# Attention and two feed-forward layers on one core: the second chunk's keys through GpSimd, keys ahead of queries, the second weight by halves

## The chip, the cores and the metric

The kernel runs on one core of a Trainium2 chip. The metric is device time in microseconds (us), median of several executions; lower is better. The core has five engines that each carry out their own list of instructions in order: TensorE (PE, matrix products), VectorE (DVE), ScalarE (ACT), GpSimd (POOL) and SyncE (SP, which here only issues DMAs). An engine waits at an instruction until the semaphores that it names are there, and everything behind it in that engine's list waits too.

## What is computed

```python
def _attn_ref(q, k, v):                       # (8, 8, 576, 64) each
    q_s = np.exp(q - np.max(q, axis=-1, keepdims=True))
    q_s = q_s / (np.sum(q_s, axis=-1, keepdims=True) + 1e-09)
    k_s = np.exp(k - np.max(k, axis=2, keepdims=True))
    k_s = k_s / (np.sum(k_s, axis=2, keepdims=True) + 1e-09)
    kv = np.einsum('bhsd,bhse->bhde', k_s, v)
    return np.einsum('bhsd,bhde->bhse', q_s, kv).astype(np.float32)

def _moe_ref(x, w_in, w_out):                 # x (4608, 512), d_ff 2048
    h = x @ w_in
    return (np.maximum(0.01 * h, h) @ w_out).astype(np.float32)

def _moe2_ref(x, w1, w2, w3, w_out):          # d_ff 768
    h = np.maximum(np.maximum(x @ w1, x @ w2), x @ w3)
    return (h @ w_out).astype(np.float32)
```

The weights come as float64, so a kernel reads them as pairs of 32-bit words. Queries are normalised along the 64 numbers of a head, keys along the 576 rows of the sequence.

## The kernel before

The 4608 rows are cut into nine chunks of 512. Attention makes the rows of a chunk (`x`), the first layer (A) takes them through 16 slices of its weights (`m` = 0 to 15), the second layer (B) follows at the end. Products are made from a high and a low half of each operand, three products for one (`mm3`, L639).

**Units.** A batch `b` has four key units (`kv_unit`), one for each pair of heads `hp`, and a chunk `c` has four query units (`q_unit`). A key unit loads keys `ke` and values `vt` (L400, L404 or L451), finds the maximum of each column of the keys over all rows, takes the exponential, multiplies keys by values (L461) and puts the result, divided by the sums, into `plain` (L471). A query unit loads `qt` (L513), finds maxima and sums along each head (L534 to L557), transposes `qt` on PE (L563), copies the transposed tile to `qf` (L565) and multiplies it by `plain` (L571). `split_x` then makes the halves of `x`: the high one on ACT (L613), the low one partly through a product of PE with minus the high half (L619) and a copy by ACT (L620), partly by DVE (L623). A unit is a generator: each `yield` ends a stage, and `advance` or `background` takes every unit one stage further.

**The maxima of keys.** In the first two batches PE transposes the keys (L415, five products a unit), and DVE finds the maxima along the free axis (L420, L421). In batch 0 the exponential is taken on the transposed tile; in batch 1 (`b == 1`) the maxima are put on a diagonal (L426) and spread over partitions by a product with the all-ones tile `ones` (L429), before DVE adds them to the keys (L431). From batch 2 on DVE takes maxima of the five key blocks (L444, L446), GpSimd's `partition_all_reduce` (L447) does it over partitions, and DVE subtracts (L452).

**Order at the start.** Units of batch 0 and chunk 0 run first, then weight 0 is converted, then the units of chunk 1 take two stages, and their others stand around step 0 of the loop over `turns`. A step is one slice `m` for one chunk: project (L639, 12 products into one PSUM tile), `g` (L917, ACT), `split_g` (L659 ACT, L660 DVE), `background(step)`, then `a_out` of the step before (12 products). The first steps are chunk 0 with m=0, then chunk 1 with m=0 and 1, then chunk 0 with m=1, 2, 3.

**Weights.** Each slice is converted by `split_words`: ACT takes the absolute value into the one scratch tile `ca` (L172, `Abs`), DVE works on it (L173 to L175), ACT writes the high half (L177), DVE goes on (L178, L179, L184) and writes the low half (L185), ACT copies a part back (L188) and issues its store (L189). `ca` has one buffer, so the conversions follow one another. `conv_a(m, after)` of slices 3 to 15 is called at steps `BEGUN` = (0, 0, 0, 2, 3, 5, 7, ... 25), and L171 has it wait for that step's `g`.

**Values.** From chunk 3 on (`CONV` = 3) the units take the number n = 4(b − 3) + hp. Their values go to a tile `vt` of a pool with one buffer, or to the tile `plain`, which is free by then: `plain` for odd n above 2.

**What sets the order.** The tile scheduler orders the instructions of each engine when the program is built; `pin` holds some in the order of the code. So an edit in one place can move instructions elsewhere.

Of the kernel before, what the change touches and what calls it, by code (L numbers as in the profile page):

```python
# [71 lines left out]
def tile_kernel(ctx: ExitStack, tc: tile.TileContext, q, k, v, wa, wb, out):  # L72
# [34 lines left out]
    def psum():  # L107
        return ps.tile([P, N], F32, tag="ps", name="ps")
# [13 lines left out]
    ones = const.tile([P, P], F32, name="ones")  # L122
# [32 lines left out]
    def split_words(raw, hi, lo, n, after=None, whole=None, keep=None):  # L155
# [30 lines left out]
        if keep is not None:  # L186
            copy = raw.bitcast(F32)[:, :N]
            nc.scalar.activation(copy, af[:, :N], AF.Copy)  # L188
            pin(nc.scalar.dma_start(keep, copy))  # L189

# [165 lines left out]
    nc.gpsimd.memset(plain, 0.0)  # L356
    spares = {}
# [26 lines left out]
    def kv_unit(b, hp, early):  # L384
# [22 lines left out]
        if b < FIRST:  # L407

            t4, t1 = (ps_acc.tile([P, N], F32, tag="acc", name="t") if i == b == 0 else psum() for i in range(2))
# [13 lines left out]
            if b == 1:  # L423

                diag = ap.tile([P, P], F32, tag="mx", name="diag", bufs=2)
                nc.scalar.activation(diag, ident, AF.Copy, scale=mx[:, 0:1])  # L426
                yield
                spread = psum()
                nc.tensor.matmul(spread[:, :P], lhsT=ones, rhs=diag, start=True, stop=True)  # L429
                yield  # L430
                nc.vector.tensor_tensor(ke, ke, spread[:, None, :P].to_broadcast([P, RK, P]), op=ALU.add)  # L431
                nc.scalar.activation(ke, ke, AF.Exp)
            else:
                nc.scalar.activation(back[:, :N], t4, AF.Exp, bias=mx[:, 0:1])
                nc.scalar.activation(back[:, N:], t1[:, :P], AF.Exp, bias=mx[:, 0:1])
                yield
                transposes()
                yield
                nc.scalar.activation(back[:, :N], t4, AF.Copy)
                nc.scalar.activation(back[:, N:], t1[:, :P], AF.Copy)  # L440
        else:
            mx = ap.tile([P, P], F32, tag="mx", name="mx", bufs=2)
            behind_step(mx[:, 0:1])
            nc.vector.tensor_tensor(mx, ke[:, 0], ke[:, 1], op=ALU.max)  # L444
            for r in range(2, RK):
                nc.vector.tensor_tensor(mx, mx, ke[:, r], op=ALU.max)  # L446
# [4 lines left out]
            fetch.dma_start(vt, v[b, hp])  # L451
# [54 lines left out]
    def q_unit(c, hp, early):  # L506
# [52 lines left out]
        qf = ap.tile([P, N], F32, tag=("qf", "qhi", "qlo")[hp % 3] if early else "qf", name="qf", bufs=1)  # L559
# [171 lines left out]

    def plan_units(c):
# [643 lines left out]
```

## Time and profile before

| | |
|---|---|
| median of three runs | 1404.0 us (1402.93, 1404.0, 1405.25) |
| profiled execution | 1404.38 us, of which the span from the first to the last instruction is 1402.6 us |
| busy over the span | PE 1380.4 us (98%), DVE 866.1 (62%), ACT 673.7 (48%), POOL 156.1 (11%) |
| chain that ended last | PE 91%, DVE 5%, ACT 2%, issue 1%, DMA 1% |
| granted TensorE clock | 0.997 of full speed as a mean |

How to read it: a share of the span says how much work an engine has, not what the time hangs on. PE is busy almost throughout, so time is lost or won where PE is not busy, or where its clock is granted at a lower level. The start (to 53.4 us) and the stretch of the weights' conversion (to some 200 us) are read by stretches and timelines below.

### The profile page before, as it was taken

The page shows a single profiled execution, that of the slowest core. Times are in us where ns is not written, and L with a number is a line of the kernel's source. Part 1 is how long each engine was busy: PE and PEld are TensorE (multiplying, and loading weights), DVE is VectorE, ACT ScalarE, POOL GpSimd, SP SyncE. Part 2 cuts the span into 40 slices and gives each one's busy share as a digit, 9 for nine tenths or more (in the row PEclk, how much of TensorE's full clock was granted, in tenths as well). Part 3 has the DMA queues.
Part 4 walks back from the last instruction along what each step waited for, and adds up shares of the span by engine and source line. Part 5 has one row for each costly group of instructions (what it writes and reads, how often), then busy time and mean ns, then how long its engine had stood idle before and what let it go on. Part 6 is the DMA issues. An engine that isn't in the chain of part 4 may idle for free.

```text
span 1402.6 us, 18333 instructions
## 1 busy us (share of the span) xinstructions
PE 1380.4 (98%) x6624; PEld 1129.5 (81%) x6624; DVE 866.1 (62%) x1500; ACT 673.7 (48%) x1387; POOL 156.1 (11%) x261
## 2 busy tenths in 40 slices
PE   7999999999999999999999999999999999999998
PEld 5788877888888788888888888888888888888887
DVE  9888977864786884656647455666457255434311
ACT  7766867753776755655445344334224223322211
POOL 0000202200112130210223200110010000000000
PEclk9999999999999999999999999999999999999999
DMA  9388864635977966768788797664674573454601
GB/s 368 129 282 302 302 225 131 199 101 213 381 291 272 374 207 230 284 219 348 243 336 335 275 372 259 243 226 172 219 268 136 210 293 120 169 221 157 235 29 38
DMA packets 90826, 330.10 MB, mean 235 GB/s; under 512 B 10672, under 2 KB 27056, under 8 KB 67568
## 3 DMA queue, kind: packets, MB, share of 16 engines
q1 hardware_dynamic: 68512, 251.46, 48.7%
q0 software_dynamic: 19056, 66.98, 14.2%
q10 hardware_dynamic: 3168, 10.49, 1.9%
q8 instruction: 52, 0.85, 0.2%
q14 instruction: 38, 0.31, 0.1%
HBM read 253.66 MB, written 75.24 MB: 234 GB/s over the span
## 4 chain that ended last, share of the span: by engine, by line
PE 91%; DVE 5%; ACT 2%; issue 1%; DMA 1%; SPq 0%; DVEq 0%; POOL 0%; ACTq 0%
PE ps L867 40%; PE acc L639 35%; PE ps L639 13%; PE ps L591 1%; PE ps L461 1%; DVE glo L660 0%; DVE qmx L534 0%; DVE side L832 0%; DVE qsm L549 0%; DMA spare<-in_q_dram 0%; DMA vt<-in_v_dram 0%; DVE nmx L420 0%; DVE spare L557 0%; PE ps L571 0%; ACT qo L527 0%
## 5 line engine op out<-in xcount | busy, mean ns | idle before, releaser
L867 PE MATMUL ps<-op,group 128*128 128x512 f32 x1512 | 352.2, 389 | 0.0
L867 PEld LDWEIGHTS ps<-op,group 128*128 128x128 f32 x1512 | 283.8, 188 | 59.0 <-ACT snap L1099 0.2
L639 PE MATMUL acc<-ghi,outw 128*128 128x512 f32 x768 | 248.2, 391 | 0.9 <-ACT ghi L659 0.5
L867 PE MATMUL ps<-opA,group 128*128 128x512 f32 x1008 | 247.4, 391 | 0.6 <-ACT opA L827 0.6
L867 PEld LDWEIGHTS ps<-opA,group 128*128 128x128 f32 x1008 | 188.0, 188 | 41.1 <-ACT opA L827 1.0
L639 PEld LDWEIGHTS acc<-ghi,outw 128*128 128x128 f32 x768 | 143.8, 188 | 32.1 <-ACT ghi L659 1.6
L639 PE MATMUL acc<-glo,outw 128*128 128x512 f32 x384 | 150.6, 392 | 0.6 <-DVE glo L660 0.2
L639 PE MATMUL acc<-wo,h 128*128 128x512 f32 x558 | 135.6, 389 | 0.0
L639 PE MATMUL ps<-xhi,w 128*128 128x512 f32 x384 | 127.1, 398 | 1.3 <-ACT g L917 0.7
L639 PE MATMUL acc<-ghi,w 128*128 128x512 f32 x384 | 127.2, 394 | 0.0
L1099 ACT ACTIVATE snap<-ps 128x512 f32<-128x512 f32 x108 | 61.8, 596 | 134.6 <-PE ps L867 134.3
L639 PEld LDWEIGHTS acc<-wo,h 128*128 128x128 f32 x558 | 104.8, 188 | 21.7
L660 DVE TENSOR_TENSOR glo<-g,ghi 128x512 fp32r<-128x512 f32 x102 | 69.5, 686 | 74.4 <-ACT ghi L659 74.1
L1114 DVE TENSOR_TENSOR snap<-snap,ps 128x512 f32<-128x512 f32 x72 | 49.1, 684 | 92.8 <-ACT snap L1099 69.4
L639 PEld LDWEIGHTS ps<-xhi,w 128*128 128x128 f32 x384 | 72.8, 190 | 17.8 <-ACT g L917 1.1
L639 PEld LDWEIGHTS acc<-glo,outw 128*128 128x128 f32 x384 | 72.1, 188 | 17.2 <-DVE glo L660 2.5
L659 ACT ACTIVATE ghi<-g 128x512 fp32r<-128x512 f32 x102 | 63.4, 630 | 46.0 <-DVE g L1299 27.3
L639 PEld LDWEIGHTS acc<-ghi,w 128*128 128x128 f32 x384 | 71.9, 188 | 15.4
L1110 DVE TENSOR_TENSOR best<-snap,ps 128x512 f32<-128x512 f32 x36 | 24.7, 686 | 87.7 <-PE ps L867 38.8
L639 PE MATMUL ps<-xlo,w 128*128 128x512 f32 x192 | 75.5, 394 | 0.0
L639 PE MATMUL acc<-glo,w 128*128 128x512 f32 x192 | 75.3, 392 | 0.0
L1123 ACT ACTIVATE h<-best 128x512 fp32r<-128x512 f32 x48 | 30.3, 630 | 87.5 <-DVE best L1116 87.1
(188 smaller groups left out, 1916.0 us busy)
## 6 DMA issues: line engine op xcount, KB each, us to landing
group<-stream SPq DMA_DIRECT2D x62, 1024.0 KB, 6.6
outw<-stream_out SPq DMA_DIRECT2D x48, 1024.0 KB, 8.4
group<-stream_in SPq DMA_DIRECT2D x42, 1024.0 KB, 7.8
stream<-room POOLq DMA_DIRECT2D x66, 256.0 KB, 5.5
raw<-in_wa_dram SPq DMA_DIRECT2D x16, 1024.0 KB, 7.7
x<-st SPq DMA_DIRECT2D x40, 256.0 KB, 3.3
room<-in_wb_dram POOLq DMA_DIRECT2D x18, 512.0 KB, 8.0
stream_out<-w SPq DMA_DIRECT2D x16, 512.0 KB, 3.5
```

The lines of the kernel that those rows point to most:

```text
L461: nc.tensor.matmul(acc[z, : D + 1], lhsT=ke[:, r, z], rhs=vt[:, r, h], start=r == 0, stop=r == RK - 1)
L591: nc.tensor.matmul(both(xps, c0, c1), lhsT=a, rhs=halves(y, c0, c1), start=i == 0, stop=i == 2)
L639: nc.tensor.matmul(acc, lhsT=l, rhs=r, start=first and i == 0, stop=last and i == 2)
L659: nc.scalar.activation(hi[:, z], g[:, z], AF.Copy)
L660: nc.vector.tensor_tensor(lo[:, z], g[:, z], hi[:, z].bitcast(F32), op=ALU.subtract)
L867: nc.tensor.matmul(bank, lhsT=l, rhs=r, start=fresh and first, stop=last, skip_group_check=not fresh)
L1099: nc.scalar.activation(t, bank, AF.Copy)
L1110: nc.vector.tensor_tensor(g, snap, bank, op=ALU.add)
L1114: nc.vector.tensor_tensor(snap, snap, bank, op=ALU.add)
L1123: nc.scalar.activation(h[:, m, 0], g, AF.Copy)
```

## The change

It has five parts, all in the code for the first 230 us.

1. Keys of batch 1 no longer pass through PE. DVE takes the maximum over the five key blocks in one reduction over a strided view (L457 of the new file, `ke.rearrange("p r d -> p d r")`), GpSimd reduces over partitions (L463), DVE subtracts (L469). The 20 transposes, the diagonals and the four products with `ones` go. `ones` shrinks to one column, and a first `partition_all_reduce` on it is issued at the start (L380).
2. For chunk 1 all four key units stand ahead of the four query units in the list of units, and after step 0 the query units are taken on pair by pair.
3. The second weight (m=1) is converted by `split_by_halves`: ACT's `Abs` (L195) around step 0, then DVE does two halves of eight operations (L201 to L208; the high half too, L204), between the query units' stages. The third weight follows with the old function.
4. `qf` of chunks 0 and 1 goes back into `qt`'s place instead of three tiles of the pool.
5. Values of units n = 2, 4, 6, ... go to `plain`, where before n = 3, 5, 7, ... did.

```diff
+    def split_by_halves(raw, hi, lo, keep):
+        words = raw.bitcast(U32).rearrange("p (n t) -> p n t", t=2)
+        a = cp.tile([P, 2 * N], U32, tag="ca", name="ca")
+        pin(nc.scalar.activation(a.bitcast(F32), words[:, :, 1].bitcast(F32), AF.Abs))
+        yield
+        for i in range(2):
+            z = slice(i * N, i * N + N)
...
+            pin(nc.vector.tensor_scalar(af, af, MOST_HIGH, LEAST_HIGH, op0=ALU.min, op1=ALU.max))
...
+            nc.vector.tensor_copy(hi[:, z], af)
...
+            nc.vector.tensor_tensor(lo[:, z], af, hi[:, z].bitcast(F32), op=ALU.subtract)
+        yield
+        copy = raw.bitcast(F32)[:, :N]
+        pin(nc.scalar.activation(copy, a.bitcast(F32)[:, :N], AF.Copy))
+        pin(nc.scalar.dma_start(keep, copy))
...
+    pin(nc.gpsimd.partition_all_reduce(ones, ones, P, bass_isa.ReduceOp.max))
...
-            if n % 2 and n > 2:
+            if n > 1 and n % 2 == 0:
                 vt = plain.rearrange("p a n -> p (a n)")[:, : RK * 2 * (D + 1)]
...
-        if b < FIRST:
+        if b == 0:
...
-            if b == 1:
-
-                diag = ap.tile([P, P], F32, tag="mx", name="diag", bufs=2)
-                nc.scalar.activation(diag, ident, AF.Copy, scale=mx[:, 0:1])
-                yield
-                spread = psum()
-                nc.tensor.matmul(spread[:, :P], lhsT=ones, rhs=diag, start=True, stop=True)
-                yield
-                nc.vector.tensor_tensor(ke, ke, spread[:, None, :P].to_broadcast([P, RK, P]), op=ALU.add)
-                nc.scalar.activation(ke, ke, AF.Exp)
...
             mx = ap.tile([P, P], F32, tag="mx", name="mx", bufs=2)
...
+            if b < FIRST:
+                nc.vector.tensor_reduce(mx, ke.rearrange("p r d -> p d r"), axis=AX.X, op=ALU.max)
+            else:
+                behind_step(mx[:, 0:1])
...
-        qf = ap.tile([P, N], F32, tag=("qf", "qhi", "qlo")[hp % 3] if early else "qf", name="qf", bufs=1)
+        if c < FIRST:
+            qf = qt
+        else:
+            qf = ap.tile([P, N], F32, tag=("qf", "qhi", "qlo")[hp % 3] if early else "qf", name="qf", bufs=1)
...
-    second = advance(first_units(1), 2)
+    second = [unit(1, hp, True) for unit in (kv_unit, q_unit) for hp in range(NP)]
+    advance(second[:NP], 2)
+    advance(second[NP:], 2)
...
+            if step == 0:
+                convert = conv_by_halves(1)
+                next(convert)
             background(step)
...
             if step == 0:
-                second = advance(second, 2)
+                advance(second[:NP])
+                for hp in range(NP):
+                    advance(second[NP : NP + hp + 1], 2)
                 a_out(*prev, hold=True)
                 prev = None
-                advance(second)
+                next(convert)
+                advance(second[NP:])
+                for _ in convert:
+                    pass
                 for f in range(KDM):
                     store(f, x2[turn][:, f], accs[c][f], busy=True)
-                conv_a(1, spare(1, NP - 1))
                 conv_a(2, x_tiles(1)[0][:, NP - 1].bitcast(F32))
```

The new file's lines answer to the old ones so: L583 to L563, L585 to L565, L591 to L571, L633 to L613, L639 to L619, L640 to L620, L643 to L623, L659 to L639, L679 and L680 to L659 and L660, L689 to L669, L950 to L917, L558 to L541, L470 to L453, L488 to L471, L651 to L631, L398 to L374. L171 to L189 keep their numbers.

PE before, the end of the start-up: the products of queries and `plain` (L571), the products that make low halves of `x` (L619), and the first projection of the loop's second step (L639).

```order
L571 MATMUL ps<-qf,plain 128x2x32
L571 MATMUL ps<-qf,plain 128x2x224
L619 MATMUL ps<-xhi,kvhi_118 128x2x224 x4
L639 MATMUL ps<-xhi,w 128x512
L639 MATMUL ps<-xlo,w 128x512
L639 MATMUL ps<-xhi,w 128x512 x2
```

PE of the change at the same place:

```order
L583 MATMUL ps<-ident,spare 128x128 x4
L639 MATMUL ps<-xhi,kvhi_118 128x2x224
L591 MATMUL ps<-spare,plain 128x2x32
L591 MATMUL ps<-spare,plain 128x2x224
L659 MATMUL ps<-xhi,w 128x512
L659 MATMUL ps<-xlo,w 128x512
...
L659 MATMUL ps<-xhi,w 128x512 x2
L639 MATMUL ps<-xhi,kvhi_118 128x2x224
L659 MATMUL ps<-xhi,w 128x512 x2
```

Before, the four products for the low halves (`x4`) stood ahead of the first projection; of the change the fourth stands behind 22 products of the projections (the rows left out are 18 of these).

ACT before, from the last high half of chunk 1's `x` over the second weight's end (L188, L189) and the third weight's `Abs` (L172) to the next `g`:

```order
L613 ACTIVATE xhi<-ps 128x512
L620 ACTIVATE xlo<-ps 128x2x224 x4
L188 ACTIVATE raw<-ca 128x512
L189 DMA wi_149<-raw 128x512
L171 ACTIVATE ca<-xhi 128x1
L172 ACTIVATE ca<-raw 128x1024
L177 ACTIVATE w<-ca 128x1024
L917 ACTIVATE g<-ps 128x512 x2
```

ACT of the change there (L211 and L212 are the second weight's end):

```order
L633 ACTIVATE xhi<-ps 128x512
L640 ACTIVATE xlo<-ps 128x2x224
L211 ACTIVATE raw<-ca 128x512
L212 DMA wi_150<-raw 128x512
L171 ACTIVATE ca<-xhi 128x1
L172 ACTIVATE ca<-raw 128x1024
L950 ACTIVATE g<-ps 128x512 x2
L679 ACTIVATE ghi<-g 128x512 x2
L177 ACTIVATE w<-ca 128x1024
```

The row L640 is the copy of the product that PE now makes behind 22 others; the third weight's `Abs` stands behind it, as it stood behind the four L620. The two `g` and their high halves have moved ahead of L177.

ACT before, between the `Abs` of the twelfth weight and of the thirteenth (m = 11 and 12):

```order
L172 ACTIVATE ca<-raw 128x1024
L541 ACTIVATE qt,qsm<-qt,qmx 128x64 x8
L917 ACTIVATE g<-ps 128x512
L177 ACTIVATE w<-ca 128x1024
L669 ACTIVATE st<-acc 128x512
L659 ACTIVATE ghi<-g 128x512
L669 ACTIVATE st<-acc 128x512
L471 ACTIVATE plain<-ps,rc 64x64 x2
L669 ACTIVATE st<-acc 128x512 x2
```

ACT of the change just ahead of the twelfth weight's `Abs`:

```order
L950 ACTIVATE g<-ps 128x512
L558 ACTIVATE qt,qsm<-qt,qmx 128x64 x8
L679 ACTIVATE ghi<-g 128x512
L188 ACTIVATE raw<-ca 128x512
L689 ACTIVATE st<-acc 128x512 x4
L189 DMA wi_159<-raw 128x512
L171 ACTIVATE ca<-g 128x1
L585 ACTIVATE qf<-ps 128x512
L470 ACTIVATE ke<-ke 128x640
L172 ACTIVATE ca<-raw 128x1024
```

Before, the eight exponentials of a query unit (L541) stood behind an `Abs` and ahead of a `g`; of the change they (L558) stand between a `g` and its high half (L679), and with the stores (L689) ahead of the next `Abs`.

## Rows read from the trace of the kernel before

**Rows 1.** Stretches: us, busy PE, PEld, DVE, ACT, POOL (instructions); PEclk, DMA share, GB/s.

```profile
0.00:53.40 53.40, 41.13 (x316) 29.34 (x316) 47.90 (x121) 40.79 (x85) 3.08 (x18) 0.97 0.69 262
53.40:120.00 66.60, 66.57 (x293) 54.87 (x294) 56.64 (x65) 40.25 (x67) 0.00 (x0) 1.00 0.76 265
120.00:1402.60 1282.60, 1272.74 (x6017) 1045.33 (x6015) 761.57 (x1316) 592.64 (x1237) 153.06 (x243) 1.00 0.64 233
```

**Rows 2.** Timeline of PE: start us, duration, operation, xcount [idle before <-releaser].

```profile
52.39 0.47 PE L619 MATMUL ps<-xhi,kvhi 128*128 128x448 f32 x1 [0.66 <-ACT xhi L613]
53.43 0.50 PE L639 MATMUL ps<-xhi,w 128*128 128x512 f32 x1 [0.57 <-DVE xlo L623]
54.70 0.86 PE L639 MATMUL ps<-xhi,w 128*128 128x512 f32 x3
55.39 0.63 PE L639 MATMUL ps<-xlo,w 128*128 128x512 f32 x2
```

**Rows 3.** Groups by shape, PE, to 60 us: busy us, mean ns | idle us.

```profile
L415 PE MATMUL ps<-ident,spare 128*128 128x128 f32 x28 | 5.9, 306 | 0.1
L429 PE MATMUL ps<-diag,ones 128*128 128x128 f32 x8 | 1.8, 310 | 0.2
```

**Rows 4.** The same view of DVE, 0 to 240 us.

```profile
L660 DVE TENSOR_TENSOR glo<-g,ghi 128x512 fp32r<-128x512 f32 x32 | 22.0, 686 | 13.8 <-ACT ghi L659 13.6
L175 DVE SCALAR_TENSOR_TENSOR ca<-raw,ca 128x1024 uint32<-128x1024 uint32 x16 | 20.0, 1252 | 0.3
L184 DVE TENSOR_TENSOR ca<-ca,raw 128x1024 f32<-128x1024 f32 x16 | 19.6, 1223 | 1.1
L173 DVE TENSOR_SCALAR ca<-ca 128x1024 f32<-128x1024 f32 x16 | 11.1, 694 | 9.1 <-ACT ca L172 9.0
L452 DVE TENSOR_TENSOR ke<-ke,mx 128x640 f32<-128x640 f32 x8 | 6.4, 806 | 0.0
```

**Rows 5.** The same view of ACT, 0 to 240 us.

```profile
L659 ACT ACTIVATE ghi<-g 128x512 fp32r<-128x512 f32 x32 | 20.1, 632 | 7.1 <-PE acc L639 6.6
L172 ACT ACTIVATE ca<-raw 128x1024 f32<-128x1024 f32 x16 | 18.1, 1132 | 0.4
L669 ACT ACTIVATE st<-acc 128x512 f32<-128x512 f32 x32 | 17.1, 598 | 2.1 <-PE acc L639 1.8
L541 ACT ACTIVATE qt<-qt,qmx 128x64 f32<-128x64 f32 x32 | 10.7, 334 | 0.2 <-DVE qmx L534 0.2
L188 ACT ACTIVATE raw<-ca 128x512 f32<-128x512 f32 x16 | 10.2, 638 | 10.0 <-DVE ca L184 9.9
```

**Rows 6.** GpSimd's L447: ns min/median/max, first and last start us.

```profile
L447 POOL PARTITION_ALL_REDUCE mx<-mx x24: 656/697/2119, 135.2 to 546.4; - x24
```

**Rows 7.** First and last operation of a weight's conversion, the same view.

```profile
L172 ACT ACTIVATE ca<-raw x16: 1119/1131/1155, 16.3 to 189.5; 128x1024 f32<-128x1024 f32 x16
L185 DVE TENSOR_TENSOR w<-ca,w x16: 1206/1224/1227, 24.7 to 197.8; 128x1024 fp32r<-128x1024 f32 x16
```

**Rows 8.** Timeline of ACT: the Abs of the third, the twelfth, the thirteenth weight.

```profile
55.29 1.12 ACT L172 ACTIVATE ca<-raw 128x1024 f32<-128x1024 f32 x1
...
143.13 1.13 ACT L172 ACTIVATE ca<-raw 128x1024 f32<-128x1024 f32 x1
...
155.41 1.13 ACT L172 ACTIVATE ca<-raw 128x1024 f32<-128x1024 f32 x1
```

**Rows 9.** Timeline of PE: its two waits between 200 and 231 us.

```profile
201.75 0.50 PE L639 MATMUL ps<-xhi,w 128*128 128x512 f32 x1 [0.69 <-ACT g L917]
...
229.97 0.85 PE L461 MATMUL ps<-vt,ke 128*64 128x65 f32 x20 [2.95 <-DMA vt<-in_v_dram]
```

**Rows 10.** Busy time by stretch again, around the two places where PEclk falls.

```profile
15.50:19.00 3.50, 3.50 (x18) 3.17 (x18) 3.50 (x11) 3.50 (x8) 0.00 (x0) 0.51 1.05 394
...
227.00:230.00 3.00, 0.05 (x3) 0.06 (x3) 2.85 (x8) 2.37 (x7) 0.00 (x0) 1.00 0.72 215
230.60:234.00 3.40, 3.40 (x15) 2.63 (x11) 2.64 (x10) 1.48 (x5) 1.77 (x3) 0.50 0.55 180
```

More of the change, by code (lines that the diff above doesn't have):

```diff
@@ L121, in tile_kernel @@
         nc.vector.tensor_tensor(ident[z, z], column[z, 0], column[z, 1], op=ALU.is_equal)
-    ones = const.tile([P, P], F32, name="ones")
+    ones = const.tile([P, 1], F32, name="ones")
     nc.gpsimd.memset(ones, 1.0)
@@ L189, in split_words @@
             pin(nc.scalar.dma_start(keep, copy))
+    def split_by_halves(raw, hi, lo, keep):
[5 more added lines that the diff above has]
+            z = slice(i * N, i * N + N)
+            au, high, low = a[:, z], words[:, z, 1], words[:, z, 0]
+            af, bf = au.bitcast(F32), high.bitcast(F32)
+            pin(nc.vector.tensor_scalar(af, af, MOST_HIGH, LEAST_HIGH, op0=ALU.min, op1=ALU.max))
+            nc.vector.tensor_scalar(au, au, 3, 0x3FFFFFF8, op0=ALU.logical_shift_left, op1=ALU.bitwise_and)
+            nc.vector.scalar_tensor_tensor(au, high, 0xC0000000, au, op0=ALU.bitwise_and, op1=ALU.bitwise_or)
+            nc.vector.tensor_copy(hi[:, z], af)
+            nc.vector.tensor_scalar(high, au, 0xFF800000, None, op0=ALU.bitwise_and)
+            nc.vector.scalar_tensor_tensor(bf, low, 2.0**-52, bf, op0=ALU.mult, op1=ALU.mult)
+            nc.vector.tensor_tensor(af, af, bf, op=ALU.add)
+            nc.vector.tensor_tensor(lo[:, z], af, hi[:, z].bitcast(F32), op=ALU.subtract)
[3 more added lines that the diff above has]
+        pin(nc.scalar.dma_start(keep, copy))
     def flat(t):
@@ L406, in kv_unit @@
             yield
-        if b < FIRST:
-            t4, t1 = (ps_acc.tile([P, N], F32, tag="acc", name="t") if i == b == 0 else psum() for i in range(2))
+        if b == 0:
+            t4, t1 = (ps_acc.tile([P, N], F32, tag="acc", name="t") if i == 0 else psum() for i in range(2))
             back = ke.rearrange("p r d -> p (r d)")
@@ L730, in conv_a, with conv_by_halves @@
         wA[m] = parts(tiles[m])
+    def conv_by_halves(m):
+        raw = words.pop(m)
+        if raw.dtype != I64:
+            yield
+            yield
+            tiles[m] = weights(raw, None, whole_in[m])
+        else:
+            w = tiles[m] = wp.tile([P, 2, 2, N], F32R, tag="w", name="w")
+            yield from split_by_halves(raw, flat(w[:, 0]), flat(w[:, 1]), whole_in[m])
+        wA[m] = parts(tiles[m])
     def plan_units(c):
```

25 lines of the change are left out of this document (12 added, 13 removed).

## The prediction

> **What bounds the kernel now.** I read the stretches first. Up to 53.4 us PE is busy for 41.13 us; from there to 120 us for 66.57 of 66.60 us; behind that for 1272.74 of 1282.60 us [rows 1]. So after the start PE has hardly any waits, and time can be won in three places: the 12.3 us that PE stands idle in the start-up, work that PE no longer has to do, and two waits near 200 and 230 us. It can be lost wherever something comes late that today comes just in time.
>
> The start-up ends where the projections begin to follow each other without a gap: 53.43 us, after waits of 0.66 us for ACT and 0.57 us for DVE [rows 2]. From there a product takes 0.23 us: three begin at 54.70, and the next at 55.39 [rows 2].
>
> The waits behind the start are 0.69 us for ACT's `g` at 201.75 and 2.95 us for values at 229.97 [rows 9]. The second costs more than its length. PE did 0.05 us of work from 227 to 230, and from 230.6 to 234 its clock was granted at 0.50, the lower level (1.2 of 2.4 GHz) [rows 10]. Half of 3.4 us is 1.7 us of lost work, so this place costs 2.95 + 1.7 = 4.6 us. PEclk was 0.51 in the start-up too, from 15.5 to 19 [rows 10].
>
> Beside PE runs a second chain: the conversion of 16 weights through one scratch tile. A conversion is an `Abs` of 1.13 us, DVE operations of 0.69, 0.69, 1.25, 0.70, 1.27, 1.22 and 1.22 us (those that I have rows for: 0.69, 1.25, 1.22) [rows 4, 5]: about 8.2 us with nothing between. It runs from 16.3 to 197.8 + 1.2 = 199 us [rows 7], and the last weight is first used in the step at 201.75 [rows 9]. From the third weight's `Abs` (55.29, [rows 8]) to the last one's (189.5, [rows 7]) thirteen conversions take 134.2 us, 10.3 us each. This chain has only 2 us to spare at its end.
>
> **How I worked the sum.** I went through the changed order row by row: each instruction begins when the one ahead on its engine is through and the results it waits for are there, and lasts as long as its like in the trace of before. Done with the old order, this puts the start-up's end at 53.51 us (trace 53.43) and the product behind the wait of 0.69 us at 201.5 (trace 201.75, [rows 9]). Operations without a like: the strided maximum L457, between 0.68 (a reduction of 512 contiguous numbers) and twice 0.81 us (L452, 640 numbers, [rows 4]); I took 0.82, one number each in L452's time. GpSimd's reduction lies between 0.66 and 2.12 us; I took 0.67, as its median is 0.70 [rows 6]. Half-length DVE operations I took at 0.42 and 0.69.
>
> **Start-up, −2.1 us.** Out go 20 transposes of PE and four diagonal products, by 5.9/28 and 1.8/8 us each [rows 3]: 20 × 0.21 + 4 × 0.23 = 5.1 us busy, of which some 3 us stood on PE's way, since the transposes run into each other. In their place, DVE has four L457 (3.3 us) for eight reductions and their minima. PE now gets the first product of queries and values at 43.0 instead of 46.1 us, 3.1 us earlier. But it then goes pair by pair: product, ACT's high half (0.6), the next `qf` (0.6), next product, about 2.4 us a pair, where before the four products stood together. Of 3.1 us, 2.1 stay: projections begin at 51.3. The second weight's halves run on DVE beneath this and end at 52.8, just ahead of its first use at 52.9; the edit costs nothing here only because PE has seven projections of the first weight to do first. The removed diagonals and the place of `qf` have no other price.
>
> **Third weight late, +3.1 us.** The fourth product for a low half now stands behind 22 projections (the first pair of order excerpts shows the product, the second its copy): 51.3 + 22 × 0.23 = 56.3 us. ACT stands at its copy L640 until 56.7, with L211 (0.64), a DMA and the third weight's `Abs` queued behind. That `Abs` begins at 58.4 instead of 55.29 [rows 8]. Behind it come two `g` and two high halves (0.63 each, [rows 5]). PE is dry for 1.4 us at 59.7 (waiting for the first high half), 0.8 at 67.1 (third weight's low half) and 0.7 at 70.3 (a high half). Here the 2.1 us are gone: at 71 us PE stands 1.0 us behind before.
>
> **Chain of conversions, +10.9 us.** The `Abs` of every other weight now stands further back among ACT's rows. Ahead of the twelfth one are eight exponentials (with their sums 2.7 us in all), a high half, a copy, four stores of 0.60, a `qf` and the exponential of a key unit [rows 5]. The walk has it at 158.8 us instead of 143.13 [rows 8]. The thirteen conversions take 11.4 us each instead of 10.3: late by 3 us at the third weight, 10 at the tenth, 17 at the sixteenth, whose low half is there at 215 instead of 199 us. Up to 153 us the weights have enough to spare, and nothing shows on PE. Then it is dry for 1.6, 0.9, 0.7, 1.2 and 0.4 us between 154 and 186: the eight exponentials hold back a high half (3.2 us between `g` and L679, where L659 followed its `g` after 0.6), and a `qf` comes late. From 204 to 219 us the last two weights themselves are late: 1.2, 1.5, 2.4 and 1.6 us. Together 11.5 us, of which the 0.7 to 0.9 us at 201.75 stood in before as well. Net 10.6 to 10.9, of which I take 10.9, since the walk of the old order was early here by 0.3; PE is then 11.9 us behind.
>
> **Values, −4.6 us.** Unit n = 2 no longer waits for the single value tile, so the wait at 229.97 and the low clock behind it go [rows 9, 10]. What is late next there is a high half, 1.05 us at 239 in the walk, inside the sum below.
>
> **Clock, +1.3 us.** Between 39 and 43 us PE is dry for 3.3 us, and between 213 and 219 for 3.9. The row shows what followed such a stretch: 3.4 us at 0.50, 1.7 us lost [rows 10]. At the first place most of what follows waits for ACT anyway; I put 0.4 there and half of 1.7 at the second. Bounds 0 and 3.1.
>
> **Sum.** −2.1 + 3.1 + 10.9 − 4.6 = +7.3, plus 1.3 = +8.6. The profiled execution took 1404.4, near the median of 1404.0, so 1413 us. If all ACT and DVE durations were 3% shorter or longer, the sum would move by −1.3 or +1.2 us; both clock bounds add −1.3 to +1.8. So the forecast's own range is 1409 to 1417.
>
> **A rule against the change.** The reduction L457 reads its five numbers 512 bytes apart. In the trace a read of every second word (L175, 1.25 us) costs no more than one without gaps (L184, 1.22 us) [rows 4], which is why I took the contiguous price. The Trainium skill, SBUF — State Buffer, section Door 1: The DMA port swizzle (why `[64,N]` ≈ `[32,N]`), says that on-chip memory has lines of 16 bytes, and that every step to a new line pays a penalty unless a line is hit at least twice. L175's stride still hits a line twice, L457's does not. No run here shows such a reduction. By that rule L457 would be slower, by an amount that the page doesn't give; the first rival below is that case.
>
> **The rivals.**
> *Slower still.* L457 at 1.6 us, twice L452's, and GpSimd's reduction at its longest, 2.12 us [rows 6]: the four key units are in a row on DVE at 26 to 30 us, with the queries behind them. Walked so, the first costs 2.8 us more and the second 2.3 to 4. Time 1416 to 1420. For it: DVE is busy 47.9 of 53.4 us [rows 1]. Against it: most of L447's executions lie at 0.7.
> *No change.* The chain's lag is covered by what the weights have to spare; only the third weight's cost and one new wait in place of the old one remain: 1404.4 + 1.0 = 1405, if a late key or query transfer stands where the values stood. For it: nothing shows up to 153 us. Against it: the last weight had 2 us to spare and falls behind by 16.
> *Faster.* The order of ACT costs nothing because PE's rows run later than walked, so that the chain keeps its 10.3 us a weight: then the start-up's 2.1 and the values' 4.6 us are won, 1397.7 us. It decides at the third weight: if its `Abs` begins by 55.5 us and the twelfth's by 145. Against it: the product's place in PE's list and the exponentials' in ACT's are fixed when the program is built.
>
> **How the numbers follow.** A difference under 0.2% (2.8 us) can't be told from none. Forecast 0.62, slower still 0.16, no change 0.12, faster 0.10. So slower 0.78, same 0.12, faster 0.10. The range runs from 1404, with half of the no-change case, to 1420, the end of the dearest one; the faster case stays out.
>
> **What would show it.** Projections without a gap from about 51.3 us, the third `Abs` at about 58 us, the twelfth near 159, the last low half near 215; PE dry at 60, 67, 154 to 186 and 204 to 219 us; no wait for values near 230 to 245. Wrong would be a chain that ends by 205 us, or L457 well above 0.82 us.

## The result, and the profile after

The changed kernel took 1419.6 us (median of 1417.11, 1419.37, 1419.83 and 1420.17), the old one 1404.2 us beside it: a ratio of 1.0105, with a 95% interval of 1.0093 to 1.0117. It is slower by 15.4 us. The forecast was 1413 us and slower; the range (1404 to 1420) holds the median, at its upper end; the forecast's own range, 1409 to 1417, does not. The profiled execution is the fastest of the four, 1417.1 us with a span of 1414.9 us, 12.3 us longer than before.

Stretches of the changed kernel, cut as in [rows 1] (us, PE's busy time and instructions, PEclk, DMA share, GB/s):

```profile
0.00:53.40 53.40, 40.51 (x288) 0.97 0.70 267
53.40:120.00 66.60, 64.08 (x279) 1.00 0.65 224
120.00:1414.90 1294.90, 1278.72 (x6033) 1.00 0.64 232
37.60:40.60 3.00, 3.00 (x7) 0.50 0.00 0
```

PE was idle for 0.03 us between 53.4 and 120 us before, and is now for 2.5. Behind 120 us it was idle for 9.9 us and is now for 16.2. The start-up's PE work fell by 0.6 us only, for 28 instructions fewer. The low clock (0.50, 37.6 to 40.6 us) is no reason for that, since the start-up had as long a stretch of it before, from 15.5 to 19 us [rows 10]; why the work that stayed takes longer was not taken apart.

What ended PE's waits between 56 and 260 us (us in all, times, longest); before there were two, of 0.7 and 2.9 us [rows 9]:

```profile
PE ps L659 <- DVE w L185: 4.0, 3, 2.1
PE acc L659 <- ACT ghi L679: 3.1, 3, 1.3
PE ps L583 <- ACT raw L188: 1.5, 1, 1.5
PE ps L591 <- DVE xlo L645: 1.4, 1, 1.4
PE ps L478 <- ACT ke L470: 1.0, 1, 1.0
PE acc L659 <- ACT st L689: 0.9, 1, 0.9
PE ps L659 <- ACT g L950: 0.5, 1, 0.5
```

The wait for values (2.95 us) is gone. Waits of seven other kinds have come, 12.4 us in all, of which 7.1 are for low halves of weights (`w L185`) and high halves of `g`.

The third weight: ACT around the last pair of chunk 1's `x` and the third weight's `Abs` (start us, duration us, operation [idle before <-releaser]).

```profile
53.91 0.60 ACT L633 ACTIVATE xhi<-ps 128x512 fp32r<-128x512 f32 x1 [0.71 <-PE ps L591]
59.12 0.54 ACT L640 ACTIVATE xlo<-ps 128x448 fp32r<-128x448 f32 x1 [4.60 <-PE ps L639]
...
60.95 1.12 ACT L172 ACTIVATE ca<-raw 128x1024 f32<-128x1024 f32 x1
```

ACT stands for 4.60 us at L640, the copy of the product that PE makes behind 22 projections. The `Abs` of the third weight begins at 60.95 instead of 55.29 us [rows 8].

Between the `Abs` of the eleventh and of the twelfth weight, the place of the third pair of order excerpts:

```profile
145.14 1.13 ACT L172 ACTIVATE ca<-raw 128x1024 f32<-128x1024 f32 x1
...
153.35 0.60 ACT L950 ACTIVATE g<-ps 128x512 f32<-128x512 f32 x1
...
156.50 0.62 ACT L679 ACTIVATE ghi<-g 128x512 fp32r<-128x512 f32 x1
...
158.01 1.54 ACT L689 ACTIVATE st<-acc 128x512 f32<-128x512 f32 x3
...
160.01 0.74 ACT L470 ACTIVATE ke<-ke 128x640 f32<-128x640 f32 x1
160.64 1.12 ACT L172 ACTIVATE ca<-raw 128x1024 f32<-128x1024 f32 x1
```

The row at 153.35 is a `g`, its high half comes at 156.50, with eight exponentials between. The `Abs` behind all that begins at 160.64 us; of the same weight it began at 143.13 before [rows 8].

First and last operation of the conversions ([rows 7] before) and the strided maximum (ns min/median/max, first and last start us):

```profile
L172 ACT ACTIVATE ca<-raw x15: 1115/1124/1164, 16.5 to 208.0; 128x1024 f32<-128x1024 f32 x15
```

```profile
L457 DVE TENSOR_REDUCE mx<-spare x4: 1233/1278/1300, 24.4 to 30.9; 128x128 f32<-128x640 f32 x4
```

### The profile page after: what moved, and what is told of

Read it like the earlier page. It is cut to its first block, busy times and chain, and to the rows that moved or that the text cites. A ratio compares the mean times of both kernels' runs of the same rounds, so it can differ in the third digit from the quotient of the medians.

```text
span 1414.9 us, 18278 instructions
## 1 busy us (share of the span) xinstructions
PE 1383.3 (98%) x6596; PEld 1126.3 (80%) x6596; DVE 866.3 (61%) x1501; ACT 672.5 (48%) x1381; POOL 161.1 (11%) x266
## 4 chain that ended last, share of the span: by engine, by line
PE 89%; DVE 4%; ACT 3%; issue 2%; DMA 1%; SPq 0%; ACTq 0%; POOL 0%; DVEq 0%; POOLq 0%
PE ps L900 40%; PE acc L659 34%; PE ps L659 12%; PE ps L611 1%; PE ps L478 1%; DMA plain<-in_v_dram 1%; PE ps L591 1%; DVE glo L680 0%; DVE side L865 0%; ACT g L950 0%; DVE mx L457 0%; DVE raw L179 0%; ACT ghi L679 0%; DMA spare<-in_q_dram 0%; DVE qmx L551 0%
## 5 line engine op out<-in xcount | busy, mean ns | idle before, releaser
L900 PEld LDWEIGHTS ps<-op,group 128*128 128x128 f32 x1512 | 283.6, 188 | 59.2 <-ACT snap L1139 0.2
L659 PE MATMUL acc<-ghi,outw 128*128 128x512 f32 x768 | 248.1, 391 | 0.8 <-ACT ghi L679 0.5
L659 PEld LDWEIGHTS acc<-ghi,outw 128*128 128x128 f32 x768 | 143.7, 188 | 32.2 <-ACT ghi L679 1.6
L659 PE MATMUL acc<-glo,outw 128*128 128x512 f32 x384 | 150.5, 392 | 0.6 <-DVE glo L680 0.2
L659 PE MATMUL acc<-wo,h 128*128 128x512 f32 x558 | 135.6, 389 | 0.0
L659 PE MATMUL ps<-xhi,w 128*128 128x512 f32 x384 | 128.1, 400 | 4.4 <-DVE w L185 4.0
L659 PE MATMUL acc<-ghi,w 128*128 128x512 f32 x384 | 127.7, 397 | 4.5 <-ACT ghi L679 3.5
L659 PEld LDWEIGHTS acc<-wo,h 128*128 128x128 f32 x558 | 104.7, 188 | 21.8
L680 DVE TENSOR_TENSOR glo<-g,ghi 128x512 fp32r<-128x512 f32 x102 | 69.8, 689 | 66.1 <-ACT ghi L679 65.7
L659 PEld LDWEIGHTS ps<-xhi,w 128*128 128x128 f32 x384 | 72.4, 189 | 21.8 <-DVE w L185 5.5
L659 PEld LDWEIGHTS acc<-ghi,w 128*128 128x128 f32 x384 | 71.9, 190 | 22.0 <-ACT ghi L679 5.5
L659 PEld LDWEIGHTS acc<-glo,outw 128*128 128x128 f32 x384 | 72.1, 188 | 17.3 <-DVE glo L680 2.5
L679 ACT ACTIVATE ghi<-g 128x512 fp32r<-128x512 f32 x102 | 63.4, 629 | 40.5 <-DVE g L1339 27.3
L1150 DVE TENSOR_TENSOR best<-snap,ps 128x512 f32<-128x512 f32 x36 | 24.7, 686 | 86.8 <-PE ps L900 37.6
L659 PE MATMUL acc<-glo,w 128*128 128x512 f32 x192 | 76.0, 396 | 0.0
L659 PE MATMUL ps<-xlo,w 128*128 128x512 f32 x192 | 75.4, 393 | 0.0
```

The lines of the kernel that those rows point to most:

```text
L659: nc.tensor.matmul(acc, lhsT=l, rhs=r, start=first and i == 0, stop=last and i == 2)
L679: nc.scalar.activation(hi[:, z], g[:, z], AF.Copy)
L680: nc.vector.tensor_tensor(lo[:, z], g[:, z], hi[:, z].bitcast(F32), op=ALU.subtract)
L900: nc.tensor.matmul(bank, lhsT=l, rhs=r, start=fresh and first, stop=last, skip_group_check=not fresh)
L1150: nc.vector.tensor_tensor(g, snap, bank, op=ALU.add)
```

## Where the time went

I compared the starts of the same product (512 columns, L639 before, L659 after) in several traces. "Again" and "third" are two more executions of the changed kernel, taken with the experiments; e9 is explained below. Times in us.

| product | before | changed | again | third | e9 |
|---|---|---|---|---|---|
| 25th (start-up over) | 53.4 | 53.4 | 55.1 | 56.5 | 54.5 |
| 97th (third weight in use) | 70.1 | 73.6 | 75.4 | 76.7 | 74.2 |
| 451st | 151.3 | 155.0 | 156.7 | 158.1 | 156.1 |
| 701st (behind the last weight) | 218.6 | 234.2 | 237.1 | 237.5 | 235.5 |
| 901st | 278.3 | 290.6 | 293.5 | 293.9 | 294.3 |
| last | 1398.0 | 1410.3 | 1413.6 | 1413.6 | 1413.9 |

Behind the 901st product nothing more is lost or won, to 0.1 us (0.5 us in "again"). So the difference between the traces lies in the first 290 us, and the table gives each stage's share for the first trace of the change: −0.1 in the start-up, +3.6 at the third weight, nothing for 80 us, +11.9 up to the last weight, −3.3 at the values; +12.3 in all.

The theories that the experiments were to tell apart:
- **A, the order on ACT.** The third weight's `Abs` stands behind L640. That makes the scheduler's further order another one, in which high halves and weights come late.
- **B, DVE's work.** Four strided maxima and sixteen half-length operations are too much in a start-up where DVE is busy for 47.9 of 53.4 us [rows 1].
- **C, the clock.** PE's gaps in the start-up bring stretches of low clock, and these differ between executions.

## Experiments

### The last low half by DVE (e1)

```diff
-        if c < FIRST:
+        if c < FIRST and (c, hp) != (1, NP - 1):
```

in `split_x` of the changed kernel.

> The changed kernel, but the low half of the last pair of chunk 1 (hp 3) is made by DVE alone, so that PE has no fourth product for it and ACT no copy (L640) to wait at. Theory A (the order on ACT): the third weight's Abs no longer stands behind that copy. It begins at about 54 us instead of 60, the twelfth's at about 145 instead of 160, PE's dry places at 63, 70, 158, 178 and 186 us go, and the time falls by some 11 to 12 us, to 1406 to 1408 us (from 1419.6). Theory B (DVE has too much to do in the start-up, with four strided maxima of 1.28 us and the halves of the second weight): DVE gets one more operation, so the time stays or grows by up to 1 us, 1419 to 1421 us.

Measured: 1409.8 us, a ratio to the old kernel of 1.0035 (1.0024 to 1.0045); 9.8 us less than the changed kernel. A holds, by a little less than it said, and B falls: DVE had more to do. The third `Abs` begins here:

```profile
55.82 0.60 ACT L633 ACTIVATE xhi<-ps 128x512 fp32r<-128x512 f32 x1 [0.72 <-PE ps L591]
56.44 0.63 ACT L211 ACTIVATE raw<-ca 128x512 f32<-128x512 f32 x1
...
57.72 1.12 ACT L172 ACTIVATE ca<-raw 128x1024 f32<-128x1024 f32 x1
```

No row waits for PE's deep product any more. From the start-up's end to the 451st product PE loses 0.6 us (1.84 to 2.41 us behind before), not 3.7, and the waits for `w L185` are gone:

```profile
PE ps L478 <- DMA vt<-in_v_dram: 1.8, 1, 1.8
PE ps L591 <- DVE xlo L645: 1.4, 1, 1.4
PE ps L478 <- ACT ke L470: 1.0, 1, 1.0
PE ps L659 <- ACT g L950: 0.8, 1, 0.8
PE acc L659 <- DVE glo L680: 0.5, 1, 0.5
```

What remains over the old kernel (4.2 us in the trace, 5 in the medians) is made up of the start-up, 1.8 us later with the clock at 0.50 for 6.8 us (45.5 to 52.3), and of 5.2 us between the 451st and the 701st product, new waits for values at 161 us (1.8 us) and for a low half of `x` (1.4 us) among them; the new homes of the values give 3.3 us back.

### The second weight whole (e2)

```diff
-            if step == 0:
-                convert = conv_by_halves(1)
-                next(convert)
...
+                conv_a(1, spare(1, NP - 1))
                 conv_a(2, x_tiles(1)[0][:, NP - 1].bitcast(F32))
```

> The changed kernel, but the second weight is converted by the old function, where the old kernel called it; keys by GpSimd, keys first, qf in place and the new homes stay. Theory A: what matters is where ACT's list has the third weight's Abs; here it lands at about 57 us instead of 60, behind no copy that waits for PE, and the chain keeps about 10.2 us a weight, so 1409 to 1412 us, though the projections begin 2 to 3 us later than in the changed kernel. Theory B (DVE's work): the eight operations of the old function take as long as the sixteen halves, so no more than 1 us is won, 1418 to 1420 us.

Measured: 1410.2 us, ratio 1.0034 (1.0023 to 1.0046). As A said, by another way to the same end: the third `Abs` began at 59.2 us, 1.8 us earlier than in the changed kernel though its start-up ended 4.3 us later, and PE lost nothing between 75 and 205 us. The start-up is the most of the 5 us that remain, with the clock at 0.71 of full speed as a mean from 40 to 58 us. What the half-length conversion is worth by itself this does not tell: the start-up ended at 57.7 us without it and at 53.4 to 56.5 with it, but the low clock differed too.

### The new homes alone (e3)

```diff
-            if n % 2 and n > 2:
+            if n > 1 and n % 2 == 0:
```

in the old kernel.

> The old kernel with the new homes for values alone (n = 2, 4, 6 to plain). Theory A: the wait of 2.95 us at 230 us shrinks to one of about 1 us for a high half or an exponential, and the clock doesn't fall behind it: 1404.2 - 1.9 - 1.7 = 1400.6 us, between 1399 and 1401. Rival: the values were late because the queue that loads them is, so they come as late into another tile, and the time stays at 1404.

Measured: 1403.0 us beside 1404.85, ratio 0.9984 (0.9975 to 0.9994). The part does what it says, but for less than half of my price. PE's waits from 210 to 300 us, where there was one of 2.95 us:

```profile
PE ps L461 <- ACT ke L453: 1.0, 1, 1.0
PE acc L639 <- DVE glo L660: 0.9, 1, 0.9
```

The low clock behind 230 us is gone as well (PEclk 1.00 there), yet behind the values stood the exponential of the same keys, 1.0 us later, and a low half, 0.9 us.

### Pairwise maxima (e4)

```diff
-                nc.vector.tensor_reduce(mx, ke.rearrange("p r d -> p d r"), axis=AX.X, op=ALU.max)
+                nc.vector.tensor_tensor(mx, ke[:, 0], ke[:, 1], op=ALU.max)
+                for r in range(2, RK):
+                    nc.vector.tensor_tensor(mx, mx, ke[:, r], op=ALU.max)
```

> The changed kernel, but the maximum over the five key blocks is taken by four operations on contiguous blocks (as for later batches) instead of one strided reduction of 1.28 us. Four such operations follow each other every 0.2 us in the old trace, about 0.9 us, so each unit saves some 0.4 us on DVE and the four 1.6. Theory A: the third weight's Abs stays behind the last low half, and the chain is as late as it was; the time falls by no more than 0.5 to 1 us, 1418.5 to 1419.5 us. Theory B (DVE's work in the start-up): the time falls by the full 1.6 us or more, 1418 us or less.

Measured: 1424.9 us, ratio 1.0125 (1.0100 to 1.0151). Both theories missed: less work on DVE, and 5 us more time. The trace is of the fastest of four executions, 1418.6 us with a mean granted clock of 0.997; the three others took 1424.8 to 1425.2 us at 0.990. So what it shows is not yet the 5 us. In it the chain is as late as in the changed kernel, as A said. But now that there are sixteen short operations instead of four, the scheduler puts queries' reductions between them (start us, duration, operation):

```profile
32.06 0.28 DVE L457 TENSOR_TENSOR mx<-spare 128x128 f32<-128x128 f32 x1
32.26 0.28 DVE L459 TENSOR_TENSOR mx<-mx,spare 128x128 f32<-128x128 f32 x1
32.46 0.68 DVE L565 TENSOR_TENSOR spare<-spare,qmx 128x512 f32<-128x512 f32 x1
33.06 0.28 DVE L459 TENSOR_TENSOR mx<-mx,spare 128x128 f32<-128x128 f32 x1
```

The last key unit's subtraction comes at 40.8 us, where the strided form had all maxima done by 32.1; PE waits for the exponentials behind it (3.2 and 1.5 us), is busy for 8.1 of 14 us between 36 and 50, and runs at the low clock from 42.1 to 48.9. The operation is cheaper; its place is not. Where the slower three lose another 6.5 us no trace shows; their lower granted clock makes more stretches of low clock the likely place.

### The old order of units (e5)

In the changed kernel, chunk 1's units in the old order:

```diff
-    second = [unit(1, hp, True) for unit in (kv_unit, q_unit) for hp in range(NP)]
-    advance(second[:NP], 2)
-    advance(second[NP:], 2)
+    second = advance(first_units(1), 2)
...
-                advance(second[:NP])
-                for hp in range(NP):
-                    advance(second[NP : NP + hp + 1], 2)
+                second = advance(second, 2)
...
```

> The changed kernel, but chunk 1's units stand in the old order (key unit, query unit, key unit, ...) and are taken on together as before; keys by GpSimd, the halves of the second weight, qf in place and the new homes stay. Theory A (the order on ACT): the product for the fourth low half is no longer 22 projections deep, the third weight's Abs begins at about 56 us, the chain of conversions is not late on PE, and the time falls by about 10 us, to 1408 to 1411 us (changed: 1419.6). Theory C (the start-up's clock): the time also hangs on whether PE's clock is granted low between 36 and 53 us, which costs 1.5 to 3.5 us and moves with PE's gaps there. Theory B (DVE's work in the start-up): nothing changes, 1419 us, since DVE has the same operations.

Measured: 1408.0 us, ratio 1.0024 (1.0014 to 1.0034): 11.6 us less. The third `Abs` is at 56.2 us, the start-up ends at 52.9. Three edits at different places (the last low half by DVE, e1; the second weight whole, e2; this one, e5) each bring the third weight forward, and each takes 9 to 12 us away. The strided maxima and GpSimd's part are in all three.

### The changed kernel again, twice (e6, e10)

> The changed kernel once more, for a second trace of it: its profiled execution took 1417.1 us, three others 1419.4 to 1420.2, at a granted clock of 0.994 to 0.995 instead of 0.997. Theory C: an execution of about 1419.5 has a second stretch of low clock in the start-up (between 40 and 54 us), and the projections begin 2 to 2.5 us later than 53.37, with everything behind it shifted by the same. Otherwise the difference stands at several places behind 60 us.

> The changed kernel a third time, for a third trace. Theory C: its time goes with the length of its low-clock stretches between 36 and 54 us and near 220 us; where these are as in its second trace (1420.5 us), the time is 1419 to 1421 us, where as in its first, 1417 us.

Both are the changed kernel as it is. Measured: 1420.5 and 1420.5 us. PEclk in three stretches, first in the first trace, then in the second, then in the third:

```profile
36.00:42.00 6.00, 5.33 (x32) 0.72 0.00 0
42.00:56.00 14.00, 10.51 (x47) 1.00 0.26 94
216.00:230.00 14.00, 11.29 (x50) 0.88 0.41 136
```

```profile
36.00:42.00 6.00, 3.73 (x35) 1.00 0.03 8
42.00:56.00 14.00, 10.55 (x41) 0.88 0.26 94
216.00:230.00 14.00, 10.45 (x42) 0.76 0.42 136
```

```profile
36.00:42.00 6.00, 3.73 (x40) 1.00 0.01 3
42.00:56.00 14.00, 10.62 (x36) 0.76 0.26 94
216.00:230.00 14.00, 10.45 (x42) 0.88 0.41 135
```

Behind 56 us the waits are the same in all three, to 0.1 us, but the low clock falls on other work, and in the start-up the waits move with it by up to 0.7 us. In the first it ran over products (36 to 42 us), and the pairs, from their first product at 45.38 us to the 25th projection, took 8.0 us; in the others it ran over the pairs (42 to 56), whose hand-over to ACT it stretches, and they took 9.2 and 10.5 us. The start-up ended at 55.1 and 56.5 instead of 53.4 us; 0.5 and 0.6 us of that stood ahead of the pairs, where PE's first product already came 1.4 us later (5.24 us, not 3.81). In the second the clock was low for longer at 220 us, too. C holds in the main for the size of the difference; the third execution has less of it at 220 us and more at 48.

### GpSimd's keys alone (e7)

The old kernel with the first part of the change only (`kv_unit` as in the diff, one column of `ones`, its first reduction).

> The old kernel with the keys of batch 1 by DVE's strided maximum, GpSimd and DVE's subtraction instead of PE's transposes (and the small ones tile with its first reduction at the start); old order of units, old conversion, old homes. Theory A/B: PE loses some 3 us of its own work, but DVE's four strided maxima of 1.28 us and the subtractions stand in the start-up, where PE waits; projections begin about 3 us later, near 56.5 us, and the rest runs as before: 1407 to 1408.5 us. Rival: what PE no longer does is saved, 1401 to 1402 us.

Measured: 1408.1 us, ratio 1.0027 (1.0018 to 1.0037). As A and B said: +3.3 us. The start-up ends at 58.0 us, 4.6 later, with PE busy for 37.7 of 58 us and the clock at 0.50 from 39.9 to 46.7 us, and from there to the 701st product all runs as before. Behind that 2.9 us come back: the wait near 230 us is 1.6 us here, for a `g`, with no low clock after it. In the old order of units the maxima by DVE and GpSimd are no gain: PE loses work, but it was waiting at that time anyway.

### What the parts may be worth together (e8)

The changed kernel with e1's, e4's and e5's edits:

> A version meant to keep what the parts are worth: the changed kernel with the old order of units, the last pair's low half by DVE, and pairwise maxima instead of the strided one. Theory A: projections begin near 50 us, the third weight's Abs at 52.5, the last weight's at about 193, no late weights; with the new homes about 5.6 us ahead of the old kernel at 280 us: 1399 us. With theory C's low clock in the start-up 1.5 to 3.5 us of that go: 1400.5 to 1402.5 us. Theory B: as DVE still has more work than in the old kernel, 1405 us or more.

Measured: 1403.4 us, ratio 0.9995 (0.9985 to 1.0004), no difference, so neither theory's time came. The start-up ended 2.2 us earlier (51.2), and 2.0 us of that stood unchanged at the 601st product. From there to the 701st PE loses 5.0 us, beginning at 201 us:

```profile
195.72 1.12 ACT L172 ACTIVATE ca<-raw 128x1024 f32<-128x1024 f32 x1
199.60 1.06 ACT L177 ACTIVATE w<-ca 128x1024 fp32r<-128x1024 f32 x1 [2.75 <-DVE ca L175]
200.56 0.58 ACT L950 ACTIVATE g<-ps 128x512 f32<-128x512 f32 x1
```

```profile
PE ps L661 <- ACT g L950: 2.0, 1, 2.0
```

A `g` stands behind the last weight's high half (L177), which stands behind its `Abs` and DVE. PE waits for 2.0 us instead of 0.7, the clock is low behind it (202 to 205), and at 210 us a low half of `x` is 1.4 us late, as in the other versions of the change. What the start-up wins and the new homes give (3.2 us behind the 701st product) goes there; the chain's end is 6 us later than before (last `Abs` at 195.72, before at 189.5).

### The third weight late, and nothing else (e9)

The old kernel, in which the third weight is converted two steps later:

```diff
-BEGUN = (0, 0, 0, 2, 3, 5, 7, 9, 11, 13, 15, 17, 19, 21, 23, 25)
+BEGUN = (0, 0, 2, 2, 3, 5, 7, 9, 11, 13, 15, 17, 19, 21, 23, 25)
...
-                conv_a(2, x_tiles(1)[0][:, NP - 1].bitcast(F32))
```

> The old kernel with one thing changed: the third weight is converted two steps later in the code (its Abs begins near 61 us instead of 55). Nothing of the change is in it. Theory A (a late third weight makes the planner's order of ACT a different one, and that order, not the start-up, costs the time): PE loses 2.4 us at the third weight, and then, although only this one conversion was moved, waits at the same places as the changed kernel, near 156, 179, 187, 206, 211, 216 and 220 us; the last Abs is at about 207 us instead of 189.5; with the clock low once or twice, 1415 to 1418 us, and at 230 us the wait for values stays or is replaced by one of about 1 us. Rival (the chain only has to make up 6 us, and it has room for that until 150 us): 1404.7 + 2.4 = 1407 us.

Measured: 1420.4 us, ratio 1.0111 (1.0095 to 1.0128). This is the changed kernel's result without any of its parts. The third `Abs` is at 62.4 us, the last at 209.1, and from 155 to 225 us PE's seven waits are the changed kernel's, each to 0.01 us. All of its waits, with the old line numbers (2.0 of the first row's 5.2 us are at the third weight, and the wait for values is there as before):

```profile
PE ps L639 <- DVE w L185: 5.2, 3, 2.1
PE ps L461 <- DMA vt<-in_v_dram: 2.1, 1, 2.1
PE ps L563 <- ACT raw L188: 1.5, 1, 1.5
PE ps L571 <- DVE xlo L625: 1.4, 1, 1.4
PE acc L639 <- ACT ghi L659: 1.3, 1, 1.3
PE acc L639 <- ACT st L669: 0.9, 1, 0.9
PE ps L639 <- ACT g L917: 0.5, 1, 0.5
```

ACT's rows there are those of the changed kernel too. From the `Abs` of the fourth weight to that of the sixteenth its 212 rows stand in the same order in both, by operation and shape, without one exception; of the old kernel's 210 rows no more than 152 can be found in that order. In the place of the excerpt: a `g` at 154.45, its high half at 157.61 behind eight exponentials, four stores, a `qf`, an exponential of keys and then the twelfth `Abs` at 161.75. The rival, under which a delay of one conversion costs 2.4 us and is then caught up, falls. One conversion that begins 7 us later tips the scheduler into another order, and that order costs another 12 us between 150 and 220 us.

### Later units (e11, e12)

The old kernel with the new homes, and with the units of chunks 3 and 4 begun one step later:

```diff
-HURRIED = ((24, 2), (26, 2), (28, 1), (29.5, 1), (31, 1), (32.5, 1), (34, 1), (35.5, 1))
+HURRIED = ((25, 2), (27, 2), (29, 1), (30.5, 1), (32, 1), (33.5, 1), (35, 1), (36.5, 1))
```

> The old kernel with the new homes for values, and the key and query units of chunks 3 and 4 begun one step later. In e3 two waits were left near 230 and 252 us, 1.0 us for an exponential of the keys and 0.9 for a low half. Theory A: those waits come from ACT and DVE being crowded there, and a step later both go: 1403.0 - 1.9 = 1401 us. Rival: the units are then late for their own use, and waits of 1 us or more come in place of these, 1403 to 1405 us.

Measured: 1399.6 us beside 1404.3, ratio 0.9966 (0.9954 to 0.9978). Better than A said: between the 701st and the 901st product PE takes 54.9 us instead of 59.7, and waits for nothing. The same edit without the new homes:

> The old kernel with the units of chunks 3 and 4 begun one step later, and the old homes for values. Which of the two edits of e11 (1399.6 us, 4.7 below the old kernel) won the time? If it is the later units alone, the value tile comes free before the values are asked for, the wait of 2.95 us at 230 us goes and the low clock behind it too: 1399 to 1400.5 us. If the new homes are needed with them, a wait for values of 1 to 3 us stays near 230 us: 1402 to 1404.5 us.

Measured: 1399.65 us, ratio 0.9970 (0.9959 to 0.9982). The later units are all of it. Where [rows 9] have the wait of 2.95 us, PE is never idle:

```profile
225.00:240.00 15.00, 15.00 (x102) 1.00 0.50 158
240.00:256.00 16.00, 16.00 (x109) 1.00 0.70 237
```

The values' DMA is issued no earlier than before (226.28 us; before 225.42), but PE's list has the products that need them later: they begin at 233.28 us, where before PE stood ready for them from 227.0. This version beats both kernels, by 4.4 us the old and by 20 us the changed one.

## Why the prediction was right, and where it was off

**Direction and mechanism.** Right, and shown. The size was not: 8.6 us forecast, 15.4 measured. Of the 6.8 between them 3.7 are in the first trace (1.6 in the start-up, 0.5 at the third weight, 0.2 in the chain, 1.3 at the values, by the terms with their clock), and 3.1 are what the median has over that execution. That the range holds the median is owed to its upper end, which was put there for the rival "slower still".

The deep product holds L640 (4.60 us), L640 holds the third weight's `Abs`; e9 makes the same loss with nothing but that `Abs` made late, and e1, e2 and e5 take most of it away by three different edits. The twelfth `Abs` was forecast at 158.8 us and came at 160.64; the last low half was forecast to be there at 215 and was there at 217.2.

**Start-up, −2.1 us forecast, −0.1 measured in the first trace, +1.7 and +3.0 in the others.** What failed lies ahead of the pairs, whose first product was forecast at 43.0 us:

```profile
45.38 1.24 PE L591 MATMUL ps<-spare,plain 128*128 128x64 f32 x4 [2.40 <-ACT spare L585]
```

From there the pairs took 8.0 us, where the walk had 8.3. Two terms were mis-sized. The strided maximum was taken at 0.82 us and takes 1.28: four of them are 1.8 us more on a DVE that the start-up waits for (the chain that ended last runs through all four, from 24.4 to 32.2 us). L457 well above 0.82 us was one of the prediction's own signs of being wrong. Second, the low clock: I put 0.4 us at this place, because what follows waits for ACT anyway. PE's clock was low for 3.4 us in the first trace and for 3.4 and 6.8 in the others, and because in those it falls on a chain of hand-overs between PE and ACT, it stretches that, by 1.2 and 2.5 us. One more slip changed nothing: the four diagonal products are eight rows of 0.23 us [rows 3], so 6.0 us of PE's work went and not 5.1, but the walk, not that sum, gave the term.

**The rule on strides** stood as a rival to my price. L457 reads its numbers 512 bytes apart and takes 1.28 us, where a DVE operation on as many contiguous numbers takes 0.81 [rows 4]. No run reads the same reduction without gaps, but 512 contiguous numbers took 0.68 us. The Trainium skill, SBUF — State Buffer, section Door 1: The DMA port swizzle (why `[64,N]` ≈ `[32,N]`), says that a step to a new 16-byte line pays a penalty unless a line is hit twice; the trace agrees, 1.28 us against 0.81. The rival "slower still", which put L457 at 1.6 us, was right in part in that half, and mostly wrong in the other: three of the four reductions by GpSimd took 0.70 or 0.71 us, like the median before [rows 6], and one, begun at 27.00 us while DVE's L185 ran, took 1.60 (2.34 in the third trace).

**Third weight, +3.1 forecast, +3.6 measured.** PE's dry places were as forecast, 1.35, 0.74 and 0.44 us for a high half, the third weight's low half and a high half. The deep product itself is 0.2 us. The rest is what a stop costs beyond its idle time, at the full clock (PEclk 1.00 from 53.4 to 120 us): from the product at 61.88 us to the second one after the stop, at 63.95, are 2.07 us, of which 1.35 are idle, and two products without a stop take 0.46. That makes some 0.25 us a stop, which the walk did not have.

**Chain, +10.9 forecast, +11.9 measured.** The chain fell behind as I had it: its thirteen conversions took 11.3 us each (60.95 to 207.99 us), forecast 11.4. On PE the sum agrees better than its parts. Idle time rose by 8.3 us, where 10.6 to 10.9 were forecast; up to 1.7 us is the low clock at 218 us, for which I had put half of 1.7 in another term; most of the rest is, by the same reckoning as above, what seven stops cost beyond their idle time. So the closeness is in part luck. And the argument that the lag itself is the price is only half of what e9 and e1 show. In e1 the last `Abs` begins at 201.1 us, 11.6 later than before, and PE waits for no weight. What costs is the order of ACT's rows, high halves and `g` behind exponentials and stores, and e9 has that same order from one late conversion alone; I had walked that order, so the number held.

Not all of this stage is explained by the late third weight. Between the 451st and the 701st product e1, e5 and e8 still take 4.4 to 5.2 us longer than before, though their third `Abs` begins within 3.3 us of the start-up's end (before 1.9, changed 7.6). All three convert the second weight by halves. e2 and e7, which convert it whole, take 2.0 and 0.0 us longer. No run separates the halves from the rest of these edits.

**Values, −4.6 forecast, −3.3 measured, and −1.8 by themselves.** The wait and its low clock went, as forecast; what was next late was an exponential of the keys (1.0 us) and, in e3, a low half too (0.9 us). I had named a high half of 1.05 us there, right in size, and said that the sum had it; but none of its terms holds it. With it the forecast is −3.6 us, near what was measured. The rival "no change" named a late key or query transfer; what was next late was computed, not loaded.

**The rivals.** "Faster" would have needed the third `Abs` by 55.5 us and the twelfth by 145; they came at 60.95 and 160.64. Its gain at the start is real (e8: 2.2 us) but ends at 201 us. "No change" had the lag covered by what the weights have to spare; that held up to 153 us, and not behind.

**Open.** Why the clock's low stretches lie at different places in different executions of one kernel was not tried. Parts two and four were not run by themselves in the old kernel.

## What to carry to other kernels

When one engine's list holds both a late copy and the start of a long serial chain, look at what the copy's producer is queued behind: 22 products on PE delayed 14 conversions. A scheduled order does not answer smoothly; making one conversion late by 7 us in an otherwise unchanged kernel cost 16 us, and replacing an operation by a cheaper one cost 5 in the median, though not in the execution that was traced. And a wait for a transfer can be removed from either end: moving the user a step back won 4.4 us, more than finding the data another home (1.8 us).

## What the runs showed that I had not expected

- A maximum over five blocks read 512 bytes apart took 1.28 us for 640 numbers a partition, against 0.81 us for a contiguous operation on as many.
- Three executions of one kernel had PE's clock at 0.50 in different stretches of the start-up (from 37.2, 46.3 and 46.8 us on), each behind a time in which PE was idle for some of it; the projections began at 53.4, 55.1 and 56.5 us.
